# Fifteen small ScalarE transfers meant to put the DMA engines out of step, in a GroupNorm kernel that streams at the DMA limit

## Chip, cores, metric

One core of one Trainium2 chip. The metric is the device time of one launch in microseconds, median of several runs. The span of a profile is about 1.7 us shorter than the device time, and its clock starts with the span. The profile of the kernel before has a span of 631.9 us, about 0.7 us less than its median run would have: where single profiles are compared below, before looks that much too good.

## The reference

GroupNorm over x of shape (128, 1024, 32, 16) in bfloat16, 32 groups, so 4096 rows (sample, group) of 32 x 512 elements (32 KB each):

```python
xr = x.reshape(B, G, C // G, H, W)
mu = xr.mean(axis=(2, 3, 4), keepdims=True)
var = ((xr - mu) ** 2).mean(axis=(2, 3, 4), keepdims=True)
xn = (xr - mu) / jnp.sqrt(var + 1e-5)
return xn.reshape(B, C, H, W) * g[None, :, None, None] + b[None, :, None, None]
```

134 MB are read and 134 MB written; nothing is read twice.

## The kernel before

A tile is 4 samples x 32 groups = 128 partitions of 32 KB, 4 MB; there are 32 tiles and 6 buffers. SyncE loads and stores all of x and out, in transfers of 4 MB, the first and the last tile's loads and the last two tiles' stores in quarters of 1 MB. PE sums each row by matmuls with a unit matrix, ACT sums the squares, and DVE, POOL and ACT share the scaling in place. What the change touches is the beginning:

```python
def L(i):                                   # load of tile i, issued from SyncE
    xt = xpool.tile([P, F], BF16, name="xt")
    parts = NQ if i == 0 or i >= NT - 1 else 1
    w = F // parts
    for c in range(parts):
        chain("sp", nc.sync.dma_start(
            out=xt[:, c * w : (c + 1) * w], in_=x_v[i][:, c * w : (c + 1) * w]))
    state[i] = {"xt": xt}

for i in range(min(UPFRONT, NT)):           # six tiles: 4 quarters + 5 whole loads
    L(i)

gb_b = consts.tile([G, 2, KC], BF16)
chain("act", nc.scalar.dma_start(out=gb_b[:, 0, :], in_=g_v))
chain("act", nc.scalar.dma_start(out=gb_b[:, 1, :], in_=b_v))
# ... (cut) constants, then per tile: sum, squares, scale, store, next load
```

`chain` only keeps the order within an engine. No line names a semaphore: the framework gives each transfer a completion semaphore, and puts in the waits.

Of the kernel before, what the change touches and what calls it, by code (L numbers as in the profile page):

```python
# [11 lines left out]
BF16 = mybir.dt.bfloat16  # L12
# [11 lines left out]
ACT_SHARE = 2  # L24
LAST_SHARE = 3
POOL_SHARE = 13


@with_exitstack
def kernel(  # L30
# [13 lines left out]
    nc = tc.nc  # L44
# [19 lines left out]
    x_v = x.rearrange("(t n) (g k) h w -> t (n g) (k h w)", n=NS, g=G)  # L64
# [5 lines left out]
    xpool = ctx.enter_context(tc.tile_pool(name="xpool", bufs=XBUFS))  # L70
    jpool = ctx.enter_context(tc.tile_pool(name="jpool", bufs=1))
    spool = ctx.enter_context(tc.tile_pool(name="spool", bufs=4))
    pspool = ctx.enter_context(
        tc.tile_pool(name="pspool", bufs=2, space=bass.MemoryType.PSUM)
    )
# [9 lines left out]
    def chain(key, inst):  # L85
        prev = last.get(key)
        if prev is not None:
            tc.add_manual_dep(inst.ins, prev.ins.name, nosync, reason="pipeline order")
        last[key] = inst
        return inst  # L90
# [16 lines left out]
    for i in range(min(UPFRONT, NT)):  # L107
# [2 lines left out]
    gb_b = consts.tile([G, 2, KC], BF16)  # L110
    chain("act", nc.scalar.dma_start(out=gb_b[:, 0, :], in_=g_v))
    chain("act", nc.scalar.dma_start(out=gb_b[:, 1, :], in_=b_v))
    eps_t = consts.tile([P, 1], F32)
    nc.vector.memset(eps_t[:], EPS)
    warm = consts.tile([P, 1], F32)
# [6 lines left out]
        out=eye[:],  # L122
        in_=ones_b[:],
# [8 lines left out]
        out=rep[:].rearrange("q (n a) -> q n a", n=NS),  # L132
        in_=ones_b[0:G, :].rearrange("q (n a) -> q n a", n=NS),
# [223 lines left out]
    def scale_on(key, i, k):  # L357
        st = state[i]
        span = st["xt"][:, k * HW : (k + 1) * HW]
        scl = st["scl"][:, k : k + 1]  # L360
        bia = st["bia"][:, k : k + 1]
        if key == "act":
            inst = nc.scalar.activation(  # L363
                out=span, in_=span, func=ACT.Identity, bias=bia, scale=scl
            )
        else:
            eng = nc.vector if key == "dve" else nc.gpsimd
            inst = eng.tensor_scalar(  # L368
                out=span,
                in0=span,  # L370
                scalar1=scl,
                scalar2=bia,
                op0=ALU.mult,
                op1=ALU.add,
            )
        chain(key, inst)
# [10 lines left out]
    def in_parts(i):  # L387
        return i >= NT - STORE_IN_PARTS

    def A(i):  # L390

        if not in_parts(i):
            for n in range(POOL_SHARE):
                scale_on("pool", i, KC - LAST_SHARE - POOL_SHARE + n)
            for k in range(KC - LAST_SHARE - POOL_SHARE):
                scale_on("dve", i, k)
# [63 lines left out]
```

## Time and profile before

| | before |
|---|---|
| device time, median (range, 4 runs) | 634.35 us (634.23 to 634.92) |
| span of the profile | 631.9 us |
| DMA share of sixteen engines (x loads and stores) | 99.0% |
| busiest compute engine, ACT | 85% |

The page of the kernel before: the span, the forty slices of the DMA engines' busy share (9 is 90% or more) and of the rate, and the DMA queues (packets, MB, share of sixteen engines' span; q1 is SyncE's queue, q10 ScalarE's).

```profile
span 631.9 us, 3907 instructions
...
DMA  8999999999999999999999999999999999999996
GB/s 365 431 437 423 430 431 429 431 433 431 424 430 432 431 431 429 430 433 438 428 432 429 433 431 429 430 430 433 434 431 431 430 430 432 433 426 436 433 418 271
...
q1 hardware_dynamic: 10944, 268.44, 99.0%
...
q10 hardware_dynamic: 96, 0.00, 0.0%
```

The chain of waits of the kernel before, its start (columns: start us, us, what):

```profile
0.78 3.23 DMA gb_b<-in_g_dram
4.01 0.02 issue
4.03 39.34 DMA xt<-in_x_dram
```

A load of x stands behind the transfer of g here. That looks odd, because nothing computed joins them, and it was the hint that the prediction passed over: the load waits for the *semaphore* of the transfer of g, a counter that a transfer raises when it has landed. SyncE's waits show the same (columns: who waited for whom, us in total, times, longest):

```profile
SPq L101 <- DMA xt<-in_x_dram: 1.3, 1, 1.3
...
SPq L101 <- DMA gb_b<-in_b_dram: 0.5, 1, 0.5
...
SPq L101 <- DMA gb_b<-in_g_dram: 0.2, 1, 0.2
```

The timelines of SyncE and of ScalarE in the first 20 us, before (start us, us, engine, line, operation, count; q marks the sequencer, which issues):

```profile
0.79 6.05 SPq L101 DMA_DIRECT2D xt<-in_x_dram  x9
...
0.78 0.42 ACTq L111 DMA_DIRECT2D gb_b<-in_g_dram  x1
1.23 0.44 ACTq L112 DMA_DIRECT2D gb_b<-in_b_dram  x1
1.70 1.28 ACT L116 ACT_TABLE_LOAD   x1 [1.70 <-PEq L444]
...
9.61 3.71 ACT L244 ACTIVATE ja<-xt,q 128x4096 fp8e5<-128x4096 bf16 x1 [6.41 <-DVE jd L189]
```

Readings below come from the trace's single DMA packet records, not from a printed view. *Idle* is the time within a stretch in which fewer than sixteen packets were under way, in us per engine. *Excess* is what packets of 8 or 32 KB took above their medians (0.309 and 1.213 us), per engine. *Spread* is the time between the first and the last engine's completion write of one transfer. Records carry no engine number, so engines are told apart only by their order in time. Their clock is set so that the first x packet of every run is at 2.8 us; against the landings that the semaphore events give this is about 0.6 us late, alike in all runs, so differences hold.

### The profile page before, as it was taken

The numbers are of one execution on the slowest core, as the hardware profiler recorded it, in microseconds if no ns is written. First come the engines' busy times: TensorE is split into PE (matmuls) and PEld (weight loads), VectorE is DVE, ScalarE is ACT, GpSimd is POOL, SyncE is SP. The second block draws the span as 40 slices with busy tenths as digits, with TensorE's granted clock in tenths as the row PEclk, the third lists the DMA queues.
The fourth block names the chain that finished last, engine by engine and source line by source line (L and its number), as shares of the span: only waits on it lengthen the run. The fifth ranks groups of instructions, "written<-read, shape, count | busy, mean of one in ns | idle before, by whom it ended". The sixth has DMA issues, their size and how long they took to land.

```text
span 631.9 us, 3907 instructions
## 1 busy us (share of the span) xinstructions
PE 293.1 (46%) x1025; PEld 114.4 (18%) x1025; DVE 380.2 (60%) x645; ACT 539.0 (85%) x268; POOL 346.8 (55%) x523
## 2 busy tenths in 40 slices
PE   5578604553245633456433565335553345647000
PEld 2233201221112211122111222112221112213000
DVE  1087666666676576545775457754657654577660
ACT  4589999999999897877997779977989797797960
POOL 0077666666666576544775446764557654477100
PEclk9689758766787657876678766677865788658655
DMA  8999999999999999999999999999999999999996
GB/s 365 431 437 423 430 431 429 431 433 431 424 430 432 431 431 429 430 433 438 428 432 429 433 431 429 430 430 433 434 431 431 430 430 432 433 426 436 433 418 271
DMA packets 11063, 268.70 MB, mean 425 GB/s; under 512 B 1312, under 2 KB 1312, under 8 KB 1312
## 3 DMA queue, kind: packets, MB, share of 16 engines
q1 hardware_dynamic: 10944, 268.44, 99.0%
q8 instruction: 8, 0.13, 0.1%
q14 instruction: 15, 0.12, 0.0%
q10 hardware_dynamic: 96, 0.00, 0.0%
HBM read 134.22 MB, written 134.22 MB: 425 GB/s over the span
## 4 chain that ended last, share of the span: by engine, by line
DMA 67%; ACT 15%; PE 7%; issue 4%; DVE 3%; POOL 0%; SPq 0%; DVEq 0%; ACTq 0%; POOLq 0%
DMA out_dram<-xt 42%; DMA xt<-in_x_dram 25%; ACT ja L244 13%; PE pa L166 7%; DVE xt L368 3%; ACT xt L363 2%; DMA gb_b<-in_g_dram 1%; POOL scl L337 0%; SPq L101 0%; ACT rstd L308 0%; DVE rstd L312 0%; DVE jd L189 0%; POOL shift L343 0%; DVEq L455 0%; DVE bia L324 0%
## 5 line engine op out<-in xcount | busy, mean ns | idle before, releaser
L244 ACT ACTIVATE ja<-xt,negmean 128x8192 fp8e5<-128x8192 bf16 x60 | 426.7, 7112 | 52.1 <-DVE jd L189 52.0
L166 PE MATMUL pa<-xt,eye 128*128 128x512 bf16 x976 | 281.8, 460 | 289.7 <-DMA xt<-in_x_dram 278.5
L368 DVE TENSOR_SCALAR xt<-xt,scl,bia 128x512 bf16<-128x512 bf16 x536 | 352.6, 732 | 40.0 <-POOL bia L353 40.0
L368 POOL TENSOR_SCALAR xt<-xt,scl,bia 128x512 bf16<-128x512 bf16 x390 | 308.7, 806 | 3.4 <-POOL bia L353 0.3
L166 PEld LDWEIGHTS <-eye 128*128 128x128 bf16 x1024 | 114.3, 114 | 468.5 <-DMA xt<-in_x_dram 290.6
L337 POOL TENSOR_SCALAR scl<-gb,rstd 128x32 f32<-128x32 f32 x31 | 11.2, 361 | 218.2 <-DVE rstd L312 218.2
L189 DVE TENSOR_SCALAR_CACHE_REDUCE jd<-pa 128x512 bf16<-128x512 f32 x32 | 22.0, 688 | 149.0 <-PE pa L166 149.0
L363 ACT ACTIVATE xt<-xt,bia,scl 128x512 bf16<-128x512 bf16 x98 | 72.0, 798 | 0.8 <-DVE bia L324 0.8
L244 ACT ACTIVATE ja<-xt,q 128x4096 fp8e5<-128x4096 bf16 x8 | 29.6, 3706 | 6.6 <-DVE jd L189 6.4
L312 DVE RECIPROCAL rstd<-rstd 128x1 f32<-128x1 f32 x32 | 5.1, 160 | 35.8 <-ACT rstd L308 35.8
L343 POOL TENSOR_SCALAR shift<-scl,negmean 128x32 f32<-128x32 f32 x31 | 11.2, 360 | 3.1
L216 POOL TENSOR_SCALAR off<-negmean,q 128x1 f32<-128x1 f32 x2 | 0.9, 432 | 20.5 <-DVE jd L189 20.5
L166 PE MATMUL pb<-xt,eye 128*128 128x512 bf16 x48 | 11.6, 388 | 1.0 <-DMA xt<-in_x_dram 1.0
L308 ACT ACTIVATE rstd<-s,v 128x1 f32<-128x1 f32 x30 | 8.8, 294 | 2.8
L244 ACT ACTIVATION_READ_ACCUMULATOR ja<-xt,negmean 128x1 f32 x60 | 11.2, 187 | 0.0
L353 POOL TENSOR_TENSOR bia<-shift,gb 128x32 f32<-128x32 f32 x31 | 7.8, 252 | 2.6
L308 ACT ACTIVATE rstd<-var,eps_t 128x1 f32<-128x1 f32 x2 | 0.6, 295 | 9.2 <-DVE jv L292 9.2
L273 POOL TENSOR_SCALAR v<-s 128x1 f32<-128x1 f32 x30 | 5.8, 192 | 2.5
L156 DVE COPY gb<-gb_p 128x64 f32<-128x64 f32 x1 | 0.2, 224 | 5.6 <-PE gb_p L148 5.6
L116 ACT ACT_TABLE_LOAD x1 | 1.3, 1283 | 1.7 <-PEq L444 1.7
L189 DVE DVE_READ_ACCUMULATOR jd<-pa 128x1 f32 x32 | 2.6, 81 | 0.0
L292 DVE TENSOR_SCALAR_CACHE_REDUCE jv<-sq,seed 128x4 f32<-128x4 f32 x2 | 0.4, 216 | 2.7 <-ACT ja L244 2.7
(18 smaller groups left out, 6.1 us busy)
## 6 DMA issues: line engine op xcount, KB each, us to landing
xt<-in_x_dram SPq DMA_DIRECT2D x30, 4096.0 KB, 29.3
out_dram<-xt SPq DMA_DIRECT2D x30, 4096.0 KB, 38.3
xt<-in_x_dram SPq DMA_DIRECT2D x8, 1024.0 KB, 16.5
out_dram<-xt SPq DMA_DIRECT2D x8, 1024.0 KB, 17.8
gb_b<-in_g_dram ACTq DMA_DIRECT2D x1, 2.0 KB, 3.2
gb_b<-in_b_dram ACTq DMA_DIRECT2D x1, 2.0 KB, 5.3
```

The source lines that it names most:

```text
L116: chain("act", nc.scalar.activation(out=warm[:], in_=eps_t[:], func=ACT.Sqrt))
L166: nc.tensor.matmul(out=ps[:], lhsT=eye[:], rhs=st["xt"][:, k * MMN : (k + 1) * MMN], start=(k == lo), stop=(k == hi - 1),),
L189: nc.vector.tensor_scalar(out=jd[:], in0=ps[:], scalar1=-inv_n, scalar2=seed, op0=ALU.mult, op1=ALU.add, accum_out=total[:],),
L244: nc.scalar.activation(out=ja[:, 0:w], in_=st["xt"][:, k * w : (k + 1) * w], func=ACT.Square, bias=bias, scale=scale, accum_out=sq, satura ...
L273: nc.gpsimd.tensor_scalar(out=v0[:], in0=s0[:], scalar1=inv_n, scalar2=EPS, op0=ALU.mult, op1=ALU.add,),
L308: nc.scalar.activation(out=rstd[:], in_=last_sum[:], func=ACT.Sqrt, bias=bias[:], scale=scale),
L312: chain("dve", nc.vector.reciprocal(out=rstd[:], in_=rstd[:]))
L337: nc.gpsimd.tensor_scalar(out=scl[:], in0=gam, scalar1=rstd[:], scalar2=None, op0=ALU.mult),
L343: nc.gpsimd.tensor_scalar(out=shift[:], in0=scl[:], scalar1=st["negmean"][:], scalar2=None, op0=ALU.mult,),
L353: nc.gpsimd.tensor_tensor(out=bia[:], in0=shift[:], in1=bet, op=ALU.add),
L363: inst = nc.scalar.activation(out=span, in_=span, func=ACT.Identity, bias=bia, scale=scl)
L368: inst = eng.tensor_scalar(out=span, in0=span, scalar1=scl, scalar2=bia, op0=ALU.mult, op1=ALU.add,)
```

## The change

Intent: sixteen engines that all begin a row of 32 KB at the same moment may get in each other's way. Transfer k, of k rows of 2 KB, should delay the engines by different amounts, so that they begin out of step. The destination is scratch memory that nobody reads.

```diff
+STEP = 1024
...
+    dpool = ctx.enter_context(
+        tc.tile_pool(name="dpool", bufs=1, space=bass.MemoryType.DRAM)
+    )
...
     chain("act", nc.scalar.dma_start(out=gb_b[:, 1, :], in_=b_v))
+    for k in range(1, 16):
+        step = dpool.tile([16, STEP], BF16, name=f"step{k}")
+        chain(
+            "act", nc.scalar.dma_start(out=step[0:k, :], in_=x_v[0][0:k, 0:STEP])
+        )
```

## The prediction

> **What bounds the kernel now.** The DMA engines. The page's DMA row reads 9 in nearly every slice, and the queue of x loads and output stores holds 99.0% of sixteen engines' span; ACT, the busiest compute engine, is busy 85%. In the packet records a 32 KB row takes 1.213 us (median of 7,680), an 8 KB piece 0.309 us; sixteen engines at that pace give 432 GB/s. The Trainium skill ("DMA: Bandwidth & Descriptors", "Where 436 GB/s comes from") names 435 as the ceiling; the trace agrees within 1%. Each engine carries 480 rows and 128 pieces: 480 x 1.213 + 128 x 0.309 = 621.8 us; first data comes at 2.8 us, so 625 to 626 us (with completion writes) is a floor. The span is 631.9.
>
> **Where the remaining 6 us are.** By the completion writes in the packet records the engines begin in step (the first 1 MB load ends within 0.44 us on all) and drift apart: spread 1.6 us after the seventh transfer, 2.5 after the tenth, 5 to 6 from mid-run. The last store ends on the first engine at 626.2 us, on the last at 631.5; the mean is near 628. The fastest engine never stalls (9.70 us per eight rows). The excess of packets over their medians sums to 3.3 us per engine: 0.42 in the first 10 us, 0.85 between 50 and 70 us, where stores join loads, the rest thinly over 570 us. Between 10 and 50 us, engines in step and loads only, there is almost none: being in step does not itself slow a load.
>
> **What the change adds.** Fifteen transfers, the k-th of k rows of 2 KB. By the skill (same page, "Why a DMA increments its semaphore by 16 and not by 1") k rows take the lowest-numbered k engines; no run here shows it yet, and k = 1 may differ. From the line through 8 and 32 KB a 2 KB packet should take 0.083 us, its completion write 0.009 (estimates from the trace). Engine 0 gets 15 x 0.092 = 1.4 us, the last none: phases spread over one row time. Mean cost is 120 x 0.092 / 16 = 0.7 us. ACT issues at 0.43 us each (timeline): 6.5 us, so its table load moves from 1.7 to 8.2 us, its first square from 9.6 to about 9.8: off the critical path, since tile 1 lands only at 22.8. Nothing is removed.
>
> **On the critical path.** The end is the slowest engine's end. Loss: up to 1.4 us if that is a low-numbered engine. Gain: at most its stall, 5 us; plausibly 1 to 2.5 if the two bursts come from engines in step. I expect a small net gain, sign uncertain.
>
> **Prediction.** 633.6 us, range 631.0 to 636.5. Faster by over 2%: 0.01; within 2%: 0.97; slower by over 2%: 0.02.
>
> **What would show each step.** ACT queue's packets from 96 to about 336, 0.25 MB; 2 KB packets near 0.08 us; spread on the first x loads from 0.44 to about 1.5 us; 32 KB median still 1.213; burst at 50 to 70 us smaller; last-store spread below 5.3 us if it helps, about 6.5 if the delay adds to the slowest engine. The chain of waits stays mostly stores and loads.
>
> **What would make it wrong.** Small packets much slower than 0.083 us at start-up; ACT's issues slowing SyncE's first loads; stalls that follow particular engines or addresses, not phase (no gain); or phase mattering more than the trace shows, which still could not bring over about 6 us (1%).

## More of the kernel before

The engines are nearly full from the first slice to the last, so a microsecond in which all of them are empty can be expected to cost about a microsecond.

All nine x loads are issued within 6 us of the start.

## The result

637.82 us (637.20 to 637.95, 4 runs) against 634.35: 0.5% slower, ratio 1.0052 with a 95% interval of 1.0038 to 1.0066. Ratios here are the mean time of one kernel's fast runs over that of the other's of the same rounds, so not quite the ratio of the medians quoted. The class (within 2%) was right; the time lies outside the range of 631.0 to 636.5, and the sign was wrong.

The page of the kernel after the change, the same lines:

```profile
span 636.2 us, 3898 instructions
...
DMA  8999999999999999999999999999999999999995
GB/s 306 426 436 410 413 429 442 429 431 435 429 426 429 443 429 429 430 431 427 431 443 432 429 431 431 431 430 439 437 429 433 430 430 431 437 424 433 437 415 253
...
q1 hardware_dynamic: 10944, 268.44, 98.5%
q10 hardware_dynamic: 366, 0.25, 0.1%
```

Only the first of the slices differs by much: 306 GB/s against 365. A slice is 16 us. The windows view of the two kernels, stretches at the start and the long middle (columns: stretch, its us, busy us and count of PE, PEld, DVE, ACT, POOL, then PE clock, DMA share, GB/s). Before:

```profile
8.00:18.00 10.00, 6.46 (x28) 2.68 (x27) 1.59 (x5) 8.33 (x5) 0.56 (x2) 1.00 1.03 442
60.00:600.00 540.00, 250.78 (x866) 96.94 (x864) 346.63 (x569) 485.20 (x232) 325.28 (x486) 0.71 1.00 431
```

After:

```profile
8.00:18.00 10.00, 7.87 (x28) 3.01 (x27) 0.94 (x4) 3.85 (x3) 0.00 (x0) 1.00 0.93 334
60.00:600.00 540.00, 251.27 (x864) 98.26 (x880) 345.27 (x562) 484.76 (x235) 326.36 (x488) 0.71 1.00 431
```

Between 8 and 18 us the engines move 334 GB/s instead of 442; from 60 to 600 us they move the same 431. So the time is lost once, at the start. The timelines of SyncE and ScalarE after the change, first 20 us, tell how:

```profile
0.79 16.60 SPq L105 DMA_DIRECT2D xt<-in_x_dram  x9
...
1.72 12.40 ACTq L120 DMA_DIRECT2D step<-in_x_dram  x15
14.14 1.28 ACT L125 ACT_TABLE_LOAD   x1 [14.14 <-DMA step<-in_x_dram]
...
15.55 3.69 ACT L253 ACTIVATE ja<-xt,q 128x4096 fp8e5<-128x4096 bf16 x1
```

The nine x loads, issued within 6.05 us before, now take 16.60 us. The waits of SyncE after the change name the cause:

```profile
SPq L105 <- DMA step<-in_x_dram: 12.8, 4, 5.6
```

and the chain of waits after the change begins so:

```profile
2.37 5.36 DMA step<-in_x_dram
...
9.23 6.26 DMA step<-in_x_dram
15.49 0.02 issue
15.50 0.33 SPq L105
15.83 0.04 issue
15.88 31.05 DMA xt<-in_x_dram
```

What does a load of x want of a scratch transfer? The trace's semaphore events answer. In each of the two kernels all transfers of SyncE and ScalarE count on eight semaphores, given out in turn to both queues. A transfer that takes a semaphore a second time waits until its former user has landed.

| x load | issued before | waits for | issued after | waits for |
|---|---|---|---|---|
| 1st, 2nd quarter of tile 0 | 0.79, 1.23 | nothing | 0.79, 1.23 | nothing |
| 3rd quarter | 1.70 | nothing | 7.25 | first small transfer (landed 7.23) |
| 4th quarter | 2.16 | nothing | 8.47 | fifth small transfer (8.45) |
| tile 1, 4 MB | 2.87 | nothing | 14.13 | ninth small transfer (14.11) |
| tile 2 | 3.36 | nothing | 15.50 | tenth small transfer (15.49) |
| tiles 3 to 5 | 4.03 to 6.51 | g, first quarter, b | 15.88 to 16.93 | two small transfers and the fourth quarter, landed earlier |

Before the change eleven transfers shared the eight semaphores at the start, and only the last three loads had to wait, for things that land early. After it there are twenty-six. The x loads wait for the small transfers, which land up to 6.3 us after their issue, probably because they stand behind x rows on their engines (argued, not shown). So the engines run dry in three stretches, at about 8.3 to 9.7, 12.3 to 13.3 and 15.3 to 17.2 us of the packet clock. Per engine, between 8 and 18 us:

| us per engine, 8 to 18 us | before | after |
|---|---|---|
| idle | 0.00 | 1.64 |
| excess (39 packets more than 0.15 us over their medians, beside the idle stretches; none before) | 0.00 | 1.23 |
| small packets, worked out as 120 x (0.084 + 0.009) / 16 | 0 | 0.70 |

These add up to 3.57 us. The first engine finishes tile 1's load at 22.9 us before and at 26.4 after, 3.5 later, and finishes its last store at 626.2 before and 629.8 after, again 3.6 later.

And the stagger? It came and went: the spread is 1.30 us at the end of the fourth quarter, but 0.52 one transfer later, at the end of tile 1's load (0.44 before). The last dry stretch begins as the fourth quarter ends, and engines that have run empty can begin the next load together. The excess between 45 and 80 us, which the stagger should have lessened, went from 0.91 to 1.13.

### The profile page after: what moved, and what is told of

Its sections match the earlier page's. It is cut to its first block, busy times and chain, and to the rows that moved or that the text cites. A ratio compares the mean times of both kernels' runs of the same rounds, so it can differ in the third digit from the quotient of the medians.

```text
span 636.2 us, 3898 instructions
## 1 busy us (share of the span) xinstructions
PE 291.1 (46%) x1005; PEld 114.2 (18%) x1025; DVE 379.2 (60%) x645; ACT 538.8 (85%) x268; POOL 345.4 (54%) x523
## 4 chain that ended last, share of the span: by engine, by line
DMA 67%; ACT 16%; PE 7%; issue 3%; DVE 3%; ACTq 0%; POOL 0%; SPq 0%; DVEq 0%; POOLq 0%
DMA out_dram<-xt 42%; DMA xt<-in_x_dram 23%; ACT ja L253 14%; PE pa L175 7%; DVE xt L377 3%; ACT xt L372 2%; DMA step<-in_x_dram 2%; ACTq L120 0%; SPq L105 0%; POOL scl L346 0%; ACT rstd L317 0%; DVE jd L198 0%; DVE rstd L321 0%; ACTq L116 0%; ACTq L115 0%
## 5 line engine op out<-in xcount | busy, mean ns | idle before, releaser
L175 PE MATMUL pa<-xt,eye 128*128 128x512 bf16 x956 | 277.7, 458 | 295.5 <-DMA xt<-in_x_dram 293.4
L175 PE MATMUL pb<-xt,eye 128*128 128x512 bf16 x48 | 13.5, 440 | 2.1 <-DMA xt<-in_x_dram 1.8
```

Source lines behind the costliest of these rows:

```text
L175: nc.tensor.matmul(out=ps[:], lhsT=eye[:], rhs=st["xt"][:, k * MMN : (k + 1) * MMN], start=(k == lo), stop=(k == hi - 1),),
```

## The experiments

Two theories. A: the loss is the x loads waiting for shared semaphores. B: the transfers themselves (bytes, number, or the stagger) cost it. Ten kernels, five rounds each, all correct. They ran in three batches, each on another chip, with "before" measured in the same rounds: 634.49, 634.25 and 634.81 us for the first four, the next four and the last two.

### 1. The same transfers on a semaphore of their own

```diff
+    own = tc.alloc_semaphore("steps")
     for k in range(1, 16):
-        step = dpool.tile([16, STEP], BF16, name=f"step{k}")
-        chain("act", nc.scalar.dma_start(out=step[0:k, :], in_=x_v[0][0:k, 0:STEP]))
+        step = nc.dram_tensor(f"step{k}", (16, STEP), BF16, kind="Internal").ap()
+        inst = nc.scalar.dma_start(out=step[0:k, :], in_=x_v[0][0:k, 0:STEP])
+        inst = inst.then_inc(own, 16)
+        tc.no_tile_sem_insts.add(inst.ins.name)
+        chain("act", inst)
...
+    seen = consts.tile([P, 1], F32)
+    chain("pool", nc.gpsimd.memset(seen[:], 0.0).wait_op(own, 240, "sem-ge"))
```

Two earlier drafts never ran (the author's account; the record has no entry for them): one did not build (the release of a scratch tile needs a framework semaphore), and one was stopped by the race check (the semaphore is cleared at the end without a wait; the memset is that wait).

> The same fifteen transfers on the ScalarE queue, but counting on a semaphore of their own, which no x load has to wait for (one small memset on POOL waits for all fifteen, at about 10 us, long before POOL is needed). Theory A (the loss is the x loads waiting for completion semaphores that the transfers share with them, so that the DMA engines run dry between 8 and 16 us): SyncE issues its nine loads within about 6 us as before, the 1.6 us per engine of idle time between 8 and 18 us falls below 0.3, the loads keep a stagger of about 1.4 us between the first and last engine at the end of the first 4 MB transfer, and the time is 633.5 to 636.0. Theory B (the transfers themselves or the stagger cost the time): 637.0 to 638.5 as after the change, with the same loads issued early.

Measured: 636.39 us, ratio 1.0029 (1.0016 to 1.0042). Its SyncE timeline and its window from 8 to 18 us:

```profile
0.79 6.36 SPq L102 DMA_DIRECT2D xt<-in_x_dram  x9
```

```profile
8.00:18.00 10.00, 8.19 (x29) 3.21 (x28) 1.59 (x5) 4.62 (x3) 0.00 (x0) 1.00 1.07 438
```

The loads are issued early again, idle falls from 1.64 to 0.04 us, the rate returns to 438 GB/s. But 1.9 us remain: the time is just above what A expected and below what B expected. The stagger is now real (spread 2.2 us at tile 1's load). The burst it was meant for did dissolve: excess between 45 and 80 us is 0.12, against 0.91. Yet new excess came at the start (0.84 and 0.45 in 0 to 18 and 18 to 45 us, against 0.42 and 0.09), and up to 80 us the sum is 1.41 us against 1.42: nothing was won. The first engine ends its last store at 626.6, the last at 634.3: a spread of 7.7 against 5.3.

### 2. Fifteen transfers with next to nothing in them

```diff
-            "act", nc.scalar.dma_start(out=step[0:k, :], in_=x_v[0][0:k, 0:STEP])
+            "act", nc.scalar.dma_start(out=step[0:16, 0:32], in_=x_v[0][0:16, 0:32])
```

> Fifteen transfers again, but each of 16 rows of 64 B, so that every engine gets the same and next to nothing (15 x 64 B): the count stays, the bytes and the stagger go. Theory A: SyncE's third load is still held back and the engines run dry, 636.5 to 638.5. Theory B: within 0.5 us of before, 634.0 to 635.0.

Measured: 638.49 us, ratio 1.0063 (1.0050 to 1.0076), 4.0 us above before, with no stagger and 15 KB of data. As A expected. Its SyncE timeline and window:

```profile
0.79 14.96 SPq L105 DMA_DIRECT2D xt<-in_x_dram  x9
```

```profile
8.00:18.00 10.00, 6.37 (x22) 2.40 (x21) 0.70 (x2) 6.01 (x5) 0.00 (x0) 0.85 0.84 330
```

### 3. Three coarse steps

```diff
-    for k in range(1, 16):
-        step = dpool.tile([16, STEP], BF16, name=f"step{k}")
+    for k in (4, 8, 12):
+        step = dpool.tile([16, 4 * STEP], BF16, name=f"step{k}")
...                                # and 4 * STEP columns in the transfer
```

> Three transfers instead of fifteen, of 4, 8 and 12 rows of 8 KB: engines 0 to 3 get 0.93 us more than 12 to 15 (3 x 0.309), in four steps, with three completion semaphores in place of fifteen. Theory A: at most 0.5 us of engine idle time at the start, the stagger survives into the 4 MB loads (spread near 1.3 us there against 0.44), 633.0 to 636.0. Theory B: the stagger alone costs most of the 3.5 us, 636.0 to 638.0. If being out of step had the value intended, the packet excess between 45 and 80 us (0.91 us per engine before) would fall below 0.4 and the time below 633.5.

Measured: 634.43 us, ratio 0.9998 (0.9984 to 1.0011). Spread 1.07 us at tile 1's load, no idle time, but the excess between 45 and 80 us is 0.92, untouched. A stagger of four coarse groups does not dissolve the burst, and costs nothing that can be measured.

### 4. The same transfers from POOL

```diff
-            "act", nc.scalar.dma_start(out=step[0:k, :], in_=x_v[0][0:k, 0:STEP])
+            "pool", nc.gpsimd.dma_start(out=step[0:k, :], in_=x_v[0][0:k, 0:STEP])
```

(moved behind POOL's two masks)

> The same fifteen transfers issued from POOL, whose transfers count on other semaphores than those of SyncE and ScalarE. Theory A: SyncE's loads are issued as before, no dry spell, 634.0 to 636.0. Theory B: 637.0 to 638.5. Which engines a small transfer falls on may differ from the ScalarE queue, so the stagger may come out uneven.

Measured: 636.79 us, ratio 1.0038 (1.0025 to 1.0050): slower than A expected, faster than B. It looks like experiment 1 in what follows: loads issued by 6.96 us, idle 0.10, spread 2.28 at tile 1's load, excess 0.08 between 45 and 80 us, last store spread 7.5. ACT begins its squares at 10.1 us here and at 14.8 in experiment 1, so the delay of ACT is not what these two have in common.

### 5. The same bytes in one even transfer

```diff
-    for k in range(1, 16): ...
+    step = dpool.tile([16, 15 * STEP // 2], BF16, name="step")
+    chain("act", nc.scalar.dma_start(out=step[:], in_=x_v[0][0:16, 0 : 15 * STEP // 2]))
```

> One transfer of 16 rows of 15 KB: the same 240 KB as the fifteen transfers, spread evenly over the engines, with one completion semaphore. By the packet rate it costs every engine 15 x 0.038 = 0.57 us and no stagger. If what is left of the loss with a semaphore of their own (1.9 us) is extra bytes, this shows most of it, 636.0 or more; if it is the stagger that the slowest engine carries to the end, this shows only the bytes: 634.8 to 635.5.

Measured: 634.72 us against 634.25, ratio 1.0008 (0.9996 to 1.0021). The bytes are worth about the 0.57 us that the packet rate gives, at the edge of what five rounds resolve. So they are not the 1.9 us of experiment 1.

### 6. One engine delayed

```diff
-    for k in range(1, 16): ...
+    step = dpool.tile([17, STEP], BF16, name="step")
+    chain("act", nc.scalar.dma_start(out=step[:], in_=x_v[0][0:17, 0:STEP]))
```

> One transfer of 17 rows of 2 KB, which should all fall on the lowest engine (17 has no divisor from 2 to 16): 17 x 0.084 = 1.43 us of work on that engine alone. If a lag given to one engine at the start is carried to the end and this engine is among the last to finish, the time rises by 0.7 to 1.5 us (635.2 to 636.0); if another engine is last by more than that, it stays within 0.4 us of before.

Measured: 633.67 us, ratio 0.9992 (0.9978 to 1.0005). One engine does lag, by 2.4 us at tile 1's load with the other fifteen within 0.3, and the last store still ends at 631.5. A likely reading, not shown, is that another engine ends later for other reasons. This run shows something else too: its last x load is held back until 13.2 us by a shared semaphore, yet no engine is idle between 8 and 18 us. So a late issue alone cost nothing here: the engines still had work.

### 7. Five empty transfers instead of fifteen

```diff
-    for k in range(1, 16):
+    for k in range(1, 6):          # and 16 rows of 64 B, as in experiment 2
```

> Five of the fifteen 64 B transfers of the earlier run. With eight completion semaphores in rotation, two for g and b, one for the first x load and five for these use all eight, so the second x load has to wait for the first of them (about 4.3 us) and the rest follow soon: a short dry spell of 0.3 to 0.8 us per engine, 634.5 to 635.5. If the cost goes with the number of transfers and not with the semaphores, a third of the 4 us, 635.8.

Measured: 635.41 us, ratio 1.0015 (1.0003 to 1.0028), 1.2 us above before: both readings were allowed. The trace is clearer than the time. The second x load is issued at 4.19 us (1.23 before), released by the transfer of g landing at 4.17, just as expected, and all nine are out by 9.5 us. Idle between 2.8 and 8 us rises from 0.27 to 0.57.

### 8. Twice the step

Experiment 1 with `STEP = 2048`.

> The fifteen transfers with a semaphore of their own and 4 KB a row instead of 2 KB: 15 x 0.167 = 2.5 us on the lowest engine, 1.3 us on the mean. If the remaining loss is the lag of the late engines carried to the end, it grows with the row: 637.0 to 639.0, last-store spread near 9 us. If it is a cost of fifteen small transfers as such, about 636.4 again.

Measured: 636.05 us, ratio 1.0028 (1.0016 to 1.0041): no more than with half the step, so the first expectation failed. The number is that of the second, a cost of fifteen small transfers as such, which experiment 9 then rules out. Looked at closely, the stagger had hardly grown: 2.70 us at tile 1's load against 2.22. The last-store spread is 7.2.

### 9. Fifteen empty transfers on a semaphore of their own

Experiment 1 with the 16 x 64 B rows of experiment 2.

> Fifteen transfers of 16 rows of 64 B with a semaphore of their own: the same instructions in the same places as the first run with a semaphore of its own, but next to no bytes and no stagger; and the same as the 64 B run without, but no shared semaphores. If sharing semaphores was all of the 4.0 us of that run, this one is within 0.5 us of before (634.0 to 634.8). If what was left (1.9 us) with a semaphore of its own is the stagger and the bytes, the same number, 634.0 to 634.8. If it is a cost of fifteen more transfers on the queue as such, whatever they carry, 635.5 to 636.5.

Measured: 634.93 us against 634.81, ratio 1.0005 (0.9992 to 1.0018). This is the cleanest pair: experiments 2 and 9 put the same fifteen transfers in the same place and differ only in whose semaphore they count on (and in one memset, and in how the scratch is allocated), and 4.0 us become 0.1 (interval -0.5 to 1.1). Fifteen transfers as such cost nothing that can be measured. Its SyncE timeline and window:

```profile
0.79 6.16 SPq L102 DMA_DIRECT2D xt<-in_x_dram  x9
```

```profile
8.00:18.00 10.00, 7.60 (x29) 2.93 (x27) 1.59 (x5) 6.61 (x5) 0.00 (x0) 1.00 1.05 429
```

In passing, its excess between 45 and 80 us is 0.21 instead of 0.91, with 0.88 instead of 0.42 before 18 us, and the time is that of before: losing the burst gains nothing here. The spread at tile 1's load is 0.55 us in this run, so the burst went without a wide stagger.

### 10. A wide stagger in three transfers

Experiment 3 with 24 KB rows (`12 * STEP`).

> Three transfers of 4, 8 and 12 rows of 24 KB: a coarse stagger of 2.7 us between engines 0 to 3 and 12 to 15, as wide as the one that the fifteen transfers left (2.2 to 2.4), without fifteen transfers. The bytes cost 1.4 us on the mean engine. If a wide stagger at the start is kept by the late engines and comes out at the end, 636.5 to 638.0, with the last store's spread above 7 us; if only the bytes count, 635.3 to 636.0 with the spread near 5.5 us as before.

Measured: 636.40 us against 634.81, ratio 1.0027 (1.0013 to 1.0041), just below what the first theory asked for (636.5). The bands were set for a before of about 634.4; with 634.81 and 1.4 us for the bytes, bytes alone give an estimate of 636.2, so the time does not tell the two apart. The last-store spread, 7.1, does speak for the first. As in experiment 6, SyncE's last x load is held back, here to 13.0 us, and no engine is idle.

### Side by side

| run | us over before | idle 8-18 | spread at tile 1 | last store, first to last engine (spread) | last engine after the mean of sixteen |
|---|---|---|---|---|---|
| before | 0 | 0.00 | 0.44 | 626.2 to 631.5 (5.3) | 3.3 |
| the change | +3.5 | 1.64 | 0.52 | 629.8 to 635.8 (6.0) | 4.0 |
| 2 count only | +4.0 | 2.05 | 0.36 | 630.5 to 636.1 (5.6) | 3.7 |
| 7 count of five | +1.2 | 0.11 | 0.99 | 627.6 to 633.3 (5.7) | 3.9 |
| 9 count only, own semaphore | +0.1 | 0.16 | 0.55 | 626.3 to 631.9 (5.6) | 3.7 |
| 5 even bytes | +0.5 | 0.00 | 0.37 | 626.8 to 632.6 (5.8) | 3.9 |
| 6 one engine | -0.6 | 0.00 | 2.38 (one) | 626.1 to 631.5 (5.4) | 3.8 |
| 3 three steps | -0.1 | 0.00 | 1.07 | 626.9 to 632.7 (5.8) | 3.7 |
| 1 own semaphore | +1.9 | 0.04 | 2.22 | 626.6 to 634.3 (7.7) | 5.1 |
| 4 from POOL | +2.3 | 0.10 | 2.28 | 627.0 to 634.4 (7.5) | 5.2 |
| 8 double step | +1.8 | 0.02 | 2.70 | 626.7 to 633.9 (7.2) | 4.9 |
| 10 wide three | +1.6 | 0.00 | 2.62 | 627.2 to 634.3 (7.1) | 5.0 |

The second column is a difference of medians of the same rounds, good to about 0.8 us; the others come from one profile each. Two separate costs stand out: idle at the start moves the first engine's end and everything after it; with a wide stagger of many engines the last one ends 4.9 to 5.2 us after the mean, against 3.3 to 4.0 in the eight other kernels.

Not all of the second cost is stagger, because a wider stagger carries more bytes. By the durations of their packets the added transfers take 0.8 us per engine in experiment 1, 1.0 in 4 and 1.4 in 8 and 10. That leaves 1.1, 1.3, 0.4 and 0.2 us, so the times of 8 and 10 are within noise of their bytes alone; that the stagger adds to them rests on the last column.

No kernel here beats the one before by more than the runs resolve, so no better version is proposed.

## Why the prediction was wrong

**The bound was right.** The engines were full, 32 KB rows kept their 1.213 us, and no ordering could bring 2%. The change stayed within 2%, as given at 0.97.

**The step that failed** is in "What the change adds": "ACT issues at 0.43 us each (timeline): 6.5 us, so its table load moves from 1.7 to 8.2 us, its first square from 9.6 to about 9.8: off the critical path", and "Nothing is removed." The added transfers were costed as bytes and as issue time, not as users of something shared. What is lost is the early issue of seven x loads, because both queues take completion semaphores from one set of eight, and with the loads held back the engines run out of work (1.64 us idle each between 8 and 18 us). Experiments 2 and 9 show it: 4.0 us with the shared set, 0.1 without. The late issue costs only where engines run dry: in experiments 6 and 10 the last load waits until 13 us too, without idle time. Experiment 1 shows it for the change itself: the dry spell is gone, and the time falls from 3.5 us over before to 1.9. The list of what would make the prediction wrong had "ACT's issues slowing SyncE's first loads", without a cause and without weight in the range. The cause could be read in the profile of before, in the load that waits for the transfer of g.

**ACT's own delay** was off as well. The issues took 0.61 to 1.13 us each and some waited, 12.4 us in all, and the first square came at 15.55 us, not 9.8. It was off the critical path all the same: the chain of waits after the change reaches ACT's squares only at 53.87 us, and experiment 9 begins its squares late too, at 12.75, and costs nothing that can be measured.

**"Phases spread over one row time"** held only for a moment: 1.30 us of spread at the fourth quarter, near the 1.5 expected, but 0.52 at tile 1's load, behind the last dry stretch. With the waits gone the stagger came, 2.2 us instead of 1.5.

**The gain, "plausibly 1 to 2.5"**, did not come. The burst between 50 and 70 us does go in experiments 1 and 4 with their fine stagger (0.12 and 0.08 us between 45 and 80 us, against 0.91). But packets run longer earlier: 0.45 and 0.36 us between 18 and 45 us, when only loads run, against 0.09. In experiment 1 the sum up to 80 us is 1.41 us against 1.42. Whether the burst comes from engines in step stays open: it also goes in experiments 7 and 9 (0.23 and 0.21) without an intended stagger, stays in experiment 10 with a spread of 2.6 us (1.01), and the change itself has it (1.13) at nearly the spread of experiment 9. The prediction had seen that loads in step show almost no excess; it did not ask whether loads out of step would.

**The loss, "up to 1.4 us if that is a low-numbered engine"**, had the right form, but in the change itself it is not what cost the time, since the stagger was gone by tile 1's load. Where a wide stagger stayed (experiments 1, 4, 8, 10), stagger and bytes together cost 1.6 to 2.3 us, and the last engine ends at least 0.9 us further behind the mean than in any other kernel. That a late start of many engines comes out at the end is consistent with this. Why it does is argued, not shown: in each run engines are hit in turn by other packets, and with half of them late it is likelier that a late one is hit. Against a simple carry-over speak experiment 6 (one engine, 2.4 us, no loss), experiment 3 (1.07 us, no loss) and experiment 8 (twice the row, no more loss). Which engine is hit when cannot be read from these records, and stays open.

**Small things.** The 2 KB packets took 0.084 us (0.083 estimated). ScalarE's queue counted 366 packets, not 336: the first small transfer, of one row, went out as sixteen packets of 128 B with sixteen completion writes, and so delayed no engine more than another. This agrees with the rule in the Trainium skill ("DMA: Bandwidth & Descriptors", "Why a DMA increments its semaphore by 16 and not by 1"), that the number of engines follows from the slowest dimension that is not 1, here 1024 elements. By the same rule 17 rows go to a single engine: the queue counted 114 packets in experiment 6, the 96 of g and b, 17 rows and one completion write. The 2.8 us for the first data was a clock 0.6 us late, which touches the floor of 625 to 626 us and nothing else.

## What to carry to other kernels

A transfer costs more than its bytes and its issue: it takes a completion semaphore, and where the framework gives these out from a small shared set, here of eight, a later transfer on another queue waits until it lands. That costs time once the engines run out of work meanwhile. So before adding small transfers at a point where large ones are issued ahead, count the transfers in flight on all queues, and look in the waits of the issuing engine for transfers that have nothing to do with the one that waits. And where engines are full from end to end, ask of a reordering what it does to the last of them, not to the mean.

## What the Trainium skill lacked or had wrong

- That completion semaphores may be a small set (eight, given out by the framework) shared by the queues of SyncE and ScalarE, and what that can cost, is on no page I found ("DMA: Bandwidth & Descriptors", "Issuing engines are not separate DMA queues", says that issuing from several engines only saves sequencer time). Here the same fifteen 64 B transfers cost 4.0 us with the shared set and 0.1 us with a semaphore of their own.
- That packets run long beside stretches in which the engines had run dry: 39 packets more than 0.15 us over their medians between 8 and 18 us after the change, none before. Whether running dry is the cause stays open: experiments 7 and 9 have 23 and 15 such packets there with 0.11 and 0.16 us of idle time. No page I found has it.
- "Runtime: NRT & Kernel Launch", "Instruction fetch mechanics", has instructions fetched in 16 KiB blocks by DMA, but not what that takes from a full DMA stream. The trace agrees on the size (8 packets of 16,384 B before) and shows each take 0.89 to 1.06 us. One x packet near each was 0.37 to 0.55 us over its median, in all seven cases after 80 us.
